# Attention steps of a fused attention and convolution kernel: one key tile at a time to the end, in place of two at a time from step 32

## The chip, the cores and the metric

The kernel runs on one core of a Trainium2 chip. The metric is device time in microseconds for one launch. The engines of the core are named as in the profile: PE is TensorE (PEld is its weight load), DVE is VectorE, ACT is ScalarE, POOL is GpSimd, SP is SyncE, which issues most DMAs here.

## The reference

Two stages, one behind the other. The first is attention in which a query sees only the keys that were routed to the same cluster; the second is a projection, a circular convolution along the sequence (written as a product of Fourier transforms), a gate and a last projection. Sizes: batch 4, 8 heads, sequence 768, head size 64, 16 clusters per head, model size 512.

```python
# q, k, v: (4, 8, 768, 64); centroids: (8, 16, 64); all float32
q_assign = argmax(einsum('bhsd,hcd->bhsc', q_n, c_n), -1)     # q_n, k_n, c_n: of length 1
k_assign = argmax(einsum('bhsd,hcd->bhsc', k_n, c_n), -1)
mask = q_assign[:, :, :, None] == k_assign[:, :, None, :]
scores = where(mask, q @ k.T / sqrt(64), -1e9)
attn = softmax(scores, -1)
x = (attn @ v).transpose(0, 2, 1, 3).reshape(4, 768, 512)

proj = x @ w_proj                                             # (512, 1536)
x1, x2, x3 = proj[..., :512], proj[..., 512:1024], proj[..., 1024:]
x2_conv = irfft(rfft(x2, axis=1) * rfft(filter_fft, axis=0), axis=1)
out = (x1 * x2_conv * x3) @ w_out                             # (4, 768, 512)
```

## The kernel before

**Groups, pairs and steps.** The 32 heads (4 batches of 8) are cut into 8 groups of four heads; two groups make a batch. A group has two pairs of heads, and a pair has six key tiles of 128. So the attention is a list of 8 x 2 x 6 = 96 steps, numbered `i` from 0 to 95, and a step is one key tile of one pair.

**A step.** `scores` (lines 383 to 392) computes for each of the two heads (`hp`) the transposed scores of one key tile against all 768 queries: two matmuls into one PSUM tile `ps` of two banks (line 387), then Exp by ACT into an SBUF tile `p` (line 391). The cluster mask is inside the matmul, since the routing's one-hot rows are appended to q and k in the tiles `aug`. There are two `ps` tiles, and eight `p` tiles that are used in turn. `values` (lines 394 to 411) multiplies by V: four matmuls in the source, eight in the profile, since the operands are float32 (line 402), with 64 columns of weights for each head, into the one PSUM tile `o`; and DVE adds `p` to a running sum per head (line 409).

**The end of a pair.** `take` lets ACT copy `o` to SBUF (lines 415 and 416). `finish` sums the denominators over the partitions on PE (line 424), sends them through DRAM to have them inverted and spread (lines 435 to 450: small DMAs, and lines 441 and 442 on DVE), scales the output on DVE (line 455), and stores it for the second stage: sum and difference on DVE (lines 488 and 489) and a bfloat16 copy on ACT (line 490).

**Routing.** `routing(n + 1)` is a generator that prepares the next group while group n is in its steps: it transposes q and k in chunks on PE (line 303), copies them on ACT (line 305) and into `aug` (lines 313 and 314), multiplies by the centroids (line 319, copied in line 321), transposes back (line 332), finds the maximum and the one-hot rows on DVE (lines 334 to 345), transposes these (line 351), and sends them into `aug` by DMA (lines 364 and 368). It yields after each chunk. It also starts the loads of the group after.

**Hyena.** The second stage of a finished batch is a generator of units too (`units`): projection (line 503), forward transform (lines 282 and 286) with DVE's products (line 554) and POOL's sums (line 557), gate (line 508, to ACT in line 568 or DVE in line 570), inverse transform (line 520) with lines 577, 537, 538 and 539, and the last projection (line 525, copied in line 587). Batches 0, 1 and 2 are interleaved with the steps from i = 32, 56 and 80 on; batch 3 comes alone at the end. In steps 0 to 6 units of table building stand in their place. All units, and routing from the second group on, share two PSUM banks `pf`.

**The order.** The order of instructions on each engine is that in which the Python code emits them. `attend(j)` emits the scores of step j for one head, then the other, and after each one it lets routing (`lead`) advance by one unit, by two on every other call where its argument `more` is true, and then lets `conv` (tables or Hyena) advance until the work done, counted in estimated microseconds, has caught up with a due time of 1.65 per `attend`. `later` and `tick` hold back things such as the end of a pair until the same count has moved on. The main loop is:

```python
if i < TWO:
    attend(i + 1, False)
    values(i)
elif i % 2 == 0:
    if i == TWO:
        attend(i + 1, True)
    attend(i + 2, True)
    attend(i + 3, True)
    values(i)
    values(i + 1)
```

With `TWO = 32`, steps 0 to 31 go one by one, with the scores one step ahead. From step 32 on, two steps of scores are emitted and then the P times V of the two steps before them, back to back: 16 matmuls of line 402 in one block.

Of the kernel before, what the change touches and what calls it, by code (L numbers as in the profile page):

```python
# [30 lines left out]
def kernel(  # L31
# [677 lines left out]
    def attend(i, more):  # L709

        due[0] += 1.65
        for hp in range(2):
            scores(i, hp)
            tick(0.35)
            calls[0] += 1
            if unit(lead) == 0.0 or (more and calls[0] % 2):
                unit(lead)
            if not conv:
                due[0] = min(due[0], paid[0] + 0.8)
            while conv and paid[0] + 0.4 < due[0] - 0.8 * (1 - hp) and unit(conv):  # L720
                pass
# [6 lines left out]
            later(2.5, pairs[n, pr].finish_on_pe if i == len(steps) - 1 else pairs[n, pr].finish)  # L728


    TWO = 32
    for hp in range(2):
        scores(0, hp)
    for i, (n, pr, sk) in enumerate(steps):
# [8 lines left out]
        if i % 24 == 8 and b > 0:  # L743
            conv.append(Hyena(b - 1, *xu[b - 1]).units())
# [6 lines that stand above are left out]
# [44 lines left out]
```

## Time and profile before

| | |
|---|---|
| median of the runs | 518.72 us (518.3 to 519.14, 2 runs) |
| the profiled execution: time, span | 518.3 us, 516.5 us |
| mean granted TensorE clock | 0.943 |
| PE busy | 421.0 us (82%) |
| DVE busy | 324.6 us (63%) |
| ACT busy | 288.8 us (56%) |
| POOL busy | 114.7 us (22%) |
| line 402, P times V on PE | 768 matmuls, 144.0 us |
| line 387, scores on PE | 384 matmuls, 94.4 us |
| line 391, Exp on ACT | 192, 153.8 us, mean 819 ns |
| line 409, sums on DVE | 160, 157.1 us |

The span runs from the first to the last instruction; the time of the execution has 1.8 us more around it. The busy time of PE is that of matmuls, which overlap a little, so that the price of a block is better read from the start of one block to the start of the next. In lines of the timeline the columns are start and length in us, engine, source line, operation, what is written and read, shapes and count; in brackets is the idle time of the engine before the line and what ended it.

### The profile page before, as it was taken

To read this page: it belongs to the slowest core of one execution; us is meant where nothing else is said; L and a number is where in the kernel's file an instruction comes from. 1 tells how busy PE (TensorE), PEld (TensorE's weight loads), DVE (VectorE), ACT (ScalarE), POOL (GpSimd) and SP (SyncE) were. 2 spreads that over 40 slices of the span, in tenths; PEclk is the share of its full clock that TensorE was granted. 3 is DMA by queue.
4 is the path that set the end of the run, shared out by engine and by line. 5 is a ranking of instruction groups with operands and counts; after the bars stand their busy time and mean duration, and the time that the engine had idled before them with its cause. 6 is when DMAs were issued, how large, how long until landed. Compare 5 with 4: busy or idle time off the path is not lost.

```text
span 516.5 us, 6689 instructions
## 1 busy us (share of the span) xinstructions
PE 421.0 (82%) x2426; PEld 184.4 (36%) x2426; DVE 324.6 (63%) x445; ACT 288.8 (56%) x475; POOL 114.7 (22%) x119
## 2 busy tenths in 40 slices
PE   4268999899796878988699876997679988978973
PEld 3133344334243433443244422443224433323521
DVE  6822887776829475565926678571683597564653
ACT  3569679679554755375456742666455736324211
POOL 7208202003006301121100413112040061111331
PEclk9669999899899898999699997999999999999988
DMA  9954827037010620135031620022004010103003
GB/s 176 237 123 93 159 76 197 19 101 171 15 49 7 148 61 33 32 92 124 30 126 32 155 63 30 1 60 65 1 32 155 2 31 0 33 0 124 1 0 122
DMA packets 67417, 38.43 MB, mean 74 GB/s; under 512 B 56060, under 2 KB 62648, under 8 KB 67384
## 3 DMA queue, kind: packets, MB, share of 16 engines
q1 hardware_dynamic: 64616, 34.99, 26.3%
q0 software_dynamic: 1056, 2.10, 2.3%
q10 hardware_dynamic: 1712, 0.92, 0.6%
q8 instruction: 19, 0.31, 0.3%
q14 instruction: 14, 0.11, 0.1%
HBM read 32.04 MB, written 7.85 MB: 77 GB/s over the span
## 4 chain that ended last, share of the span: by engine, by line
PE 53%; DVE 24%; ACT 9%; issue 7%; POOL 4%; DMA 1%; POOLq 0%; DVEq 0%; ACTq 0%; SPq 0%
PE o L402 19%; PE ps L387 8%; DVE acc L409 6%; PE pf L508 5%; ACT p L391 3%; PE pf L525 3%; PE pf L503 3%; PE pf L424 3%; DVE tm L554 2%; PE pf L303 2%; PE pf L520 2%; DVE osb L455 2%; ACT qkT L305 2%; POOL hy L539 1%; DVE mx L334 1%
## 5 line engine op out<-in xcount | busy, mean ns | idle before, releaser
L391 ACT ACTIVATE p<-ps 128x768 f32<-128x768 f32 x192 | 153.8, 819 | 81.8 <-PE ps L387 71.7
L402 PE MATMUL o<-p,vraw 128*64 128x384 f32 (+1 forms) x768 | 144.0, 512 | 0.4 <-ACT osb L416 0.4
L409 DVE TENSOR_TENSOR acc<-acc,p 128x768 f32<-128x768 f32 x128 | 123.5, 1021 | 5.1 <-ACT p L391 5.1
L387 PE MATMUL ps<-aug 128*128 128x384 bf16 (+1 forms) x384 | 94.4, 337 | 14.6 <-ACT p L391 8.0
L402 PEld LDWEIGHTS o<-p,vraw 128*64 128x64 f32 x768 | 51.6, 141 | 70.1 <-issue 68.6
L314 POOL CAST aug<-qkT 64x768 bf16<-64x768 f32 x32 | 33.0, 1035 | 133.9 <-ACT qkT L305 131.4
L387 PEld LDWEIGHTS <-aug 128*128 128x128 bf16 (+1 forms) x384 | 31.1, 99 | 77.9 <-issue 65.5
L539 POOL TENSOR_TENSOR hy<-yy,x 128x768 bf16<-128x768 f32 x12 | 25.8, 2149 | 126.5 <-DVE yy L538 126.5
L557 POOL TENSOR_TENSOR hy<-tm 128x512 bf16<-128x512 f32 x18 | 26.1, 1468 | 103.2 <-DVE tm L554 103.2
L409 DVE TENSOR_TENSOR acc<-p,p 128x768 f32<-128x768 f32 x32 | 33.6, 1087 | 21.0 <-PE pf L424 12.7
L508 PE MATMUL pf<-xT,wpj 128*128 128x384 bf16 x192 | 38.2, 330 | 7.1 <-ACT x L568 3.0
L554 DVE TENSOR_TENSOR tm<-pf,hm 128x512 f32<-128x512 f32 x36 | 22.7, 681 | 19.0 <-PE pf L282 18.1
L508 PEld LDWEIGHTS <-wpj 128*128 128x128 bf16 x256 | 24.8, 98 | 27.2 <-issue 10.7
L570 DVE TENSOR_TENSOR x<-pf,x 128x384 f32<-128x384 f32 x24 | 13.2, 555 | 31.6 <-PE pf L508 31.6
L303 PE MATMUL pf<-ident,qkraw 128*128 128x128 f32 x168 | 28.2, 286 | 5.0 <-ACT qkT L305 4.8
L305 ACT COPY qkT<-pf 128x384 f32<-128x384 f32 x56 | 26.4, 489 | 2.0 <-PE pf L303 1.7
L490 ACT CAST xT<-osb 128x768 bf16<-128x768 f32 x16 | 13.4, 835 | 24.1 <-DVE osb L455 20.1
L303 PEld LDWEIGHTS pf<-ident,qkraw 128*128 128x128 f32 x168 | 21.2, 146 | 14.4 <-ACT qkT L305 8.4
L334 DVE TENSOR_REDUCE mx<-pf 128x24 f32<-128x384 f32 x16 | 8.9, 554 | 25.6 <-PE pf L332 25.6
L520 PE MATMUL pf<-inv,hy 128*128 128x384 bf16 (+1 forms) x112 | 19.7, 338 | 5.7 <-DVE x L570 2.8
L525 PE MATMUL pf<-wout,hy 128*128 128x512 bf16 x72 | 19.6, 406 | 5.0 <-POOL hy L539 4.0
L415 ACT COPY osb<-o 128x384 f32<-128x384 f32 x16 | 7.7, 480 | 28.5 <-PE o L402 28.5
(152 smaller groups left out, 464.3 us busy)
## 6 DMA issues: line engine op xcount, KB each, us to landing
qkraw<-in_k_dram SPq DMA_DIRECT2D x32, 192.0 KB
vraw<-in_v_dram SPq DMA_DIRECT2D x8, 768.0 KB
qkraw<-in_q_dram SPq DMA_DIRECT2D x30, 192.0 KB
rb<-dr SPq DMA_DIRECT2D x30, 192.0 KB
out_dram<-tm SPq DMA_DIRECT2D x11, 512.0 KB
hy<-in_moe_filter_fft_dram SPq DMA_DIRECT2D x4, 384.0 KB
wpj<-in_moe_w_proj_dram POOLq DMA_DIRECT2D x1, 1536.0 KB, 11.5
od<-ohT SPq DMA_DIRECT2D x7, 192.0 KB
```

The source lines that it names most:

```text
L303: nc.tensor.transpose(tps[:, ts(t, 128)], qr[:, 3 * ch + t].rearrange("p h d -> p (h d)"), ident)
L305: nc.scalar.copy(qkT[z][:, ch], tps[:, :384])
L314: nc.gpsimd.tensor_copy(augs[aset][1][D:, z], qf[D:])
L387: nc.tensor.matmul(sps[:, ch, :384], self.aug[hp][:K, 2 * self.pr + 1, ts(sk, 128)], self.aug[hp][:K, 2 * self.pr, ts(ch, 384)], start=Tru ...
L391: nc.scalar.activation(p[:, :S].rearrange("p (a b) -> p a b", a=2), sps[:, :, :384], Act.Exp, scale=0.125)
L402: nc.tensor.matmul(self.o[64 * hp:64 * hp + 64, ch, :384 + ch], vv[:, 2 * self.pr + hp, sk * D:(sk + 1) * D], pb[hp][sk][:, 384 * ch:384 * ...
L409: nc.vector.tensor_tensor(acc[hp], a, pb[hp][sk][:, :S], op=Alu.add)
L508: nc.tensor.matmul(ps, wpj[:, kt, off + dt * 128:off + dt * 128 + 128], self.xT[:, kt, ts(ch, 384)], start=(kt == 0), stop=(kt == ND - 1))
L520: nc.tensor.matmul((pe, po)[e], self.y[lo:hi, i, cs, ts(dt, 128)], inv[lo:hi, row], start=(n == 0), stop=(n == 3))
L525: nc.tensor.matmul(ps, self.y2[:, kt, ts(t, 128)], wout[:, kt], start=(kt == 0), stop=(kt == ND - 1))
L539: eng.tensor_tensor(self.y2[:, dt], yy.rearrange("p t c -> p (t c)"), self.gate[dt], op=Alu.mult)
L554: nc.vector.tensor_tensor(tm[r][:, cs], ps, hm[:, i, 2 * r + cs], op=Alu.mult)
```

## The change

One constant is changed. All 96 steps take the first branch of the loop: the scores of one step, then P times V of the step before. The second branch is never entered, and `more` is always false, so routing advances by one unit per call.

```diff
-    TWO = 32
+    TWO = 96
     for hp in range(2):
         scores(0, hp)
     for i, (n, pr, sk) in enumerate(steps):
...
         if i < TWO:
             attend(i + 1, False)
             values(i)
```

On PE, what was emitted ahead of P times V of steps 36 and 37 as (S: the two score matmuls of one head, with the lines of the units between) `S 303 303 S 303 S 303 424 303 S 303 508`, then 16 of line 402, becomes `S 303 282 S 303`, eight of line 402, `424 S 303 286 S 303 286`, eight of line 402. Routing of a group then reaches its one-hot transposes (line 351) three steps later, as in the first 32 steps. The last unit of Hyena's attention-time work also shifts by a little, since the paired form calls `attend` once more at its end.

## Prediction

> **What bounds the kernel now.** I read the page first: busy shares, clock, the chain that ended last.
>
> ```profile
> PE 421.0 (82%) x2426; PEld 184.4 (36%) x2426; DVE 324.6 (63%) x445; ACT 288.8 (56%) x475; POOL 114.7 (22%) x119
> ...
> PEclk9669999899899898999699997999999999999988
> ...
> PE 53%; DVE 24%; ACT 9%; issue 7%; POOL 4%; DMA 1%; POOLq 0%; DVEq 0%; ACTq 0%; SPq 0%
> ```
>
> PE is the fullest engine and holds over half of the chain; DVE comes second. So PE time and PE waits are the currency, and the question is what the change does to each. The changed loop covers steps 32 to 95; the trace puts them at about 145 to 462 us. Over that window the windows view gives PE 267.08 us busy of 317.00, DVE 203.00, ACT 174.58: PE stands still for 49.9 us.
>
> Next, the timeline of PE in both kinds of step, for the price of a P times V block (line 402). First two single steps from the early part of the run, which has the form that the change spreads:
>
> ```profile
> 67.24 1.51 PE L402 MATMUL o<-p,vraw 128*64 128x384 f32 x8
> 68.68 0.82 PE L387 MATMUL ps<-aug 80*128 80x384 bf16 x4
> 69.44 1.51 PE L402 MATMUL o<-p,vraw 128*64 128x384 f32 x8
> ```
>
> Then a paired step, from the part that the change rewrites:
>
> ```profile
> 266.56 2.80 PE L402 MATMUL o<-p,vraw 128*64 128x384 f32 x16
> 269.30 0.50 PE L387 MATMUL ps<-aug 80*128 80x384 bf16 x2
> 269.63 1.03 PE L503 MATMUL pf<-wpj,uT 128*128 128x512 bf16 x4
> ```
>
> Read starts, not durations. A block of 8 takes 68.68 - 67.24 = 1.44 us, a block of 16 takes 269.30 - 266.56 = 2.74 us: two singles cost 0.14 us more than a pair. Two score matmuls ahead of other full-width work take 269.63 - 269.30 = 0.33 us, so four should take 0.66, but four ahead of P times V take 69.44 - 68.68 = 0.76 us: entering a block costs 0.10 us.
>
> Third, the waits of PE in 145 to 462 us, with who ended them (us in total, times, longest):
>
> ```profile
> PE pf L286 <- DVE tm L554: 7.3, 5, 2.7
> PE pf L351 <- DVE oh L345: 5.8, 4, 2.2
> PE pf L303 <- ACT qkT L305: 4.6, 8, 0.9
> PE pf L332 <- ACT sim L321: 4.0, 4, 1.0
> ...
> PE ps L387 <- ACT p L391: 2.5, 5, 0.6
> ```
>
> The whole list adds to 49.1 us in 317, or 15%. The same view over 60 to 141 us, single steps with routing but without the Hyena units, adds to only 6.1 us in 81 (7.5%), of which 3.9 is scores waiting for Exp. That wait is the one I follow last. In a single step (timeline, all engines):
>
> ```profile
> 97.13 0.83 ACT L490 CAST xT<-osb 128x768 bf16<-128x768 f32 x1 [1.94 <-DVE osb L455]
> ...
> 98.73 0.48 PE L387 MATMUL ps<-aug 80*128 80x384 bf16 x2 [1.96 <-ACT p L391]
> ```
>
> The copy of line 490 sits at the head of ACT's queue until DVE has done two sums and line 455; both Exps of the next step are queued behind it, both score buffers fill, and PE stops for 1.96 us. In a paired step the same wait is hidden:
>
> ```profile
> 376.14 2.81 PE L402 MATMUL o<-p,vraw 128*64 128x384 f32 x16
> ...
> 377.19 0.83 ACT L490 CAST xT<-osb 128x768 bf16<-128x768 f32 x1 [1.93 <-DVE osb L455]
> ...
> 378.88 0.50 PE L387 MATMUL ps<-aug 80*128 80x384 bf16 x2
> ```
>
> ACT waits as long (1.93), but PE is inside a block of 16.
>
> **The change part by part.** The base is the profiled execution, 518.3 us (span 516.5 plus 1.8 around it), 0.42 below the median of the runs, 518.72. All 96 steps become single. No matmul, Exp, sum, copy or DMA is added or removed; the order changes on every engine.
>
> *Blocks of P times V.* Steps 32 to 95 are 32 pairs, so 32 more blocks. Each costs 0.14 + 0.10 = 0.24 us: 32 x 0.24 = +7.7 us, all on PE. I see nothing that hides it where PE is busy; where PE would have waited anyway it is free, so its lower end is 0.
>
> The Trainium skill, page "TensorEngine Tiling (Array Packing)", section "Key Properties", speaks against the change: switching to another tiling mode drains the engine, and these blocks (128x64 weights) are a mode of their own between 128x128 ones. It gives no price there; "TensorE: Matmul & The Clock Gate", Part 2, puts the drain at about 128 cycles, at 2.4 GHz an estimate of 0.053 us, and two per block would make 3.4 us in place of the row's 7.7. The row decides.
>
> *Scores that wait for Exp of the same buffer.* Attending two steps in a row issues four score groups on two buffers before any P times V. Single steps put P times V between. Take the 2.5 us away; bounds -2.5 to 0.
>
> *Routing.* In pairs every other call advances routing twice, so two transposing chunks come back to back and the third waits for the copies. Waits of lines 303, 319 and 332 on ACT's copies and on line 335 add to 11.4 us in the window, and are absent from 60 to 141 us. In that stage ACT is nearly full, though (16.66 us busy of 18.30 between 76.7 and 95 us), and now Hyena's copies join, with two PSUM banks shared. I take a third back, -3.8; bounds -11.4 to 0. The one-hot transposes (line 351) waited 5.8 us in four routings; in single steps 1.8 in two. For four, -(5.8 - 3.6) = -2.2; bounds -5.8 to 0.
>
> *Routing ends later.* It is spread over three more steps, and with it go SP's loads of the next q and k, line 364 and line 368. In a single group the spread was issued at 104.1 us and the scores that need it came after 111; the new steps are longer, so there is more room. Cost 0; if the cover were gone, PE would stand still for as long as the landing is late. On SP's queue the small transfers of the divisors (435 to 450) now go between these loads; DVE already waits for them (30.0 us in the run) in places where PE mostly runs on. Cost 0, and up to +4 for four divisor waits of 1 us.
>
> *Hyena's evictions on DVE.* Sums come two at a time (1.82 us) in place of four (3.55), so an eviction queued behind them is 1.7 us less late; against that, the new DVE order puts lines 455, 488 and 489 (1.0 + 0.6 + 0.5 us) between two evictions in the gating steps, and the next inverse matmul needs both banks. Lines 282, 286, 508, 520 and 525 wait 25 us in the window; I leave that as it is, with bounds of -10 (six or so bursts shortened by 1.7) and +8 (four such places at 2.1).
>
> *Line 490 without its cover.* In the new order it comes ten times in steps 36 to 90, each time with a single block behind it. What shields PE is the other work between two score groups, priced by rows (three-matmul chunk of 332: 0.33; 282: 0.65; 508: 0.65; 503: 0.86; 520: 1.25; six of 286: 0.84). Taking 1.96 less that work, step by step: 36: 0.66; 42: 0.65; 48: 0.06; 54: 1.30; 60: 1.10; 66: 0.46; 72: 0.66; 78: 0; 84: 0.24; 90: 0.01. That is +5.1 us; bounds 0 and 10 x 1.96 = +19.6.
>
> *Clock.* Stretches in which PE worked half the time or less were followed by half clock: 95 to 99.5 us (2.33 busy), then 99.5 to 102.9 at 0.50; 191 to 195 (1.00 busy), then 195 to 198.5 at 0.51. Such a stretch costs up to 1.7 us. Both kernels have such holes; cost 0, bounds -8 and +8 (five stretches lost or gained).
>
> "TensorE: Matmul & The Clock Gate", Part 1, asks for an idle window of some 3.4 us before the clock halves; here a longest single gap of 1.96 us was enough, so by the page new short holes would cost nothing extra, and by the row they would. The row decides.
>
> Sum: +7.7 - 2.5 - 3.8 - 2.2 + 5.1 = +4.3, so 522.6 us.
>
> **The rivals.** *Line 490 bares PE* (slower). ACT in order, two score buffers, no long block. For it: 1.96 us at 98.73, and the like at 136.14 with 1.46 more on line 351 after it. Against: Hyena units now lie between. All ten bare: 19.6 in place of 5.1, 518.3 + 18.8 = 537.1 us. It decides (over +2%) from six of ten on: 6 x 1.96 = 11.8, with the other terms' -0.8 is +11.
>
> *Smoother steps* (faster). If PE's waits fell to the single stage's 7.5%: 317 - 49.1 + 7.7 = 275.6, / 0.925 = 298, so 19 less: 499.3 us. For it: halved bursts on DVE, one routing chunk per call. Against: the quiet stage has no Hyena work, and 25 us of the waits are Hyena's own.
>
> *The blocks cost nothing.* The 0.24 us falls into waits that PE has anyway: 522.6 - 7.7 = 514.9 us. For it: 15% of waits. Against: most blocks in the timeline follow PE work without a gap.
>
> **How the numbers follow.** The sum above 0.50, own range 515 to 528; blocks free 0.12; line 490 0.28; smoother 0.10. Within 2% (10.4 us, about what a measurement of this kernel can tell from no change) are the first two: 0.62; slower 0.28, faster 0.10. The range takes half of the faster case off below and goes to the full price of line 490 above: 508 to 538.
>
> **What would show it.** Right: 96 blocks of 8 with 1.44 us to the next start; the wait of scores on Exp sits after line 490 and nowhere else; lines 303 and 332 wait less than 11.4 us together. Wrong: a gap of about 2 us behind each line 490 (first rival); PE waits under 30 us in the loop (second); PE busy time that grows by 7 us while the span stays (third). A wait that I have priced nowhere, such as line 387 on a DMA, would break the sum.

## The result, and the profile after

504.31 us median (504.3 to 504.32, 2 runs) against 518.72: a ratio of 0.9722, 95% interval 0.968 to 0.9764, so 14.4 us faster. The forecast was 522.6 in a range of 508 to 538: the wrong side. The times below are medians, and each ratio is to the kernel before, run on the same chip. Its median lay between 518.7 and 521.0 us in these rounds, so a difference between two experiments is read from their ratios, as a share of 518.72 us, where it matters. Of the four runs of e3 below, two took 532 and 533 us, and its ratio is that of the other two.

The page of the changed kernel, the lines that were shown of before:

```profile
PE 420.5 (84%) x2426; PEld 179.2 (36%) x2426; DVE 336.5 (67%) x445; ACT 290.3 (58%) x475; POOL 119.2 (24%) x119
...
PEclk9769999989979898989999998999999989998998
...
PE 61%; DVE 22%; issue 6%; ACT 5%; POOL 4%; DMA 1%; POOLq 0%; DVEq 0%; SPq 0%; ACTq 0%
```

PE does the same matmuls in a shorter span (502.5 in place of 516.5 us) and now makes 61% of the chain. The waits of PE in the changed loop, 145 to 440 us:

```profile
PE pf L520 <- DVE x L570: 4.9, 5, 2.2
PE pf L282 <- DVE tm L554: 4.9, 3, 3.5
PE pf L286 <- DVE tm L554: 3.7, 2, 3.0
PE pf L286 <- DVE cand L335: 3.5, 1, 3.5
...
PE pf L508 <- DVE cand L335: 2.7, 1, 2.7
...
PE pf L332 <- DVE cand L335: 1.0, 1, 1.0
```

What has gone is routing: lines 303, 319 and 332 waited 11.4 us before and wait 1.7 now, line 351 went from 5.8 to 0.2, and the scores (line 387) from 2.5 to nothing. What has stayed are waits of Hyena's matmuls. Part of them is still owed to routing: 6.2 us of lines 286 and 508 end with line 335, which is DVE's work on routing's tile in the shared banks `pf`.

A count of PE's time over the whole span, from its records: idle 88.8 us before, 75.7 after (-13.1); work at half clock 39.2 against 34.5 us, of which half is loss (-2.3); all work, with half-clock time counted half, 401.1 against 402.8 us (+1.7). That is -13.7 of the span's -14.0. A difference of a few us in all work says little: e1 below, with the same blocks as the kernel before, has 398.1 us. By place: from the start of the block of step 31 to the start of the last matmul of line 402 the time fell from 316.7 to 298.3 us, and what comes behind it grew from 58.8 to 62.8, since single steps call `attend` once less and leave a batch of units over.

The block itself is as it was priced (231.16 to 232.60 is 1.44 us):

```profile
231.16 1.51 PE L402 MATMUL o<-p,vraw 128*64 128x384 f32 x8
232.60 0.50 PE L387 MATMUL ps<-aug 80*128 80x384 bf16 x2
```

### The profile page after: what moved, and what is told of

Read it like the earlier page. It is cut to its first block, busy times and chain, and to the rows that moved or that the text cites. A ratio compares the mean times of both kernels' runs of the same rounds, so it can differ in the third digit from the quotient of the medians.

```text
span 502.5 us, 6673 instructions
## 1 busy us (share of the span) xinstructions
PE 420.5 (84%) x2426; PEld 179.2 (36%) x2426; DVE 336.5 (67%) x445; ACT 290.3 (58%) x475; POOL 119.2 (24%) x119
## 4 chain that ended last, share of the span: by engine, by line
PE 61%; DVE 22%; issue 6%; ACT 5%; POOL 4%; DMA 1%; POOLq 0%; DVEq 0%; SPq 0%; ACTq 0%
PE o L402 22%; PE ps L387 10%; DVE acc L409 6%; PE pf L508 5%; PE pf L525 3%; PE pf L503 3%; PE pf L520 3%; DVE tm L554 3%; PE pf L424 3%; PE pf L303 3%; POOL hy L539 2%; DVE osb L455 2%; ACT p L391 2%; PE pf L319 1%; PE pf L286 1%
## 5 line engine op out<-in xcount | busy, mean ns | idle before, releaser
L402 PE MATMUL o<-p,vraw 128*64 128x384 f32 (+1 forms) x768 | 151.2, 516 | 0.4 <-ACT osb L416 0.4
L409 DVE TENSOR_TENSOR acc<-acc,p 128x768 f32<-128x768 f32 x128 | 136.7, 1113 | 6.6 <-ACT p L391 6.5
L402 PEld LDWEIGHTS o<-p,vraw 128*64 128x64 f32 x768 | 48.6, 140 | 68.7 <-issue 65.4
L314 POOL CAST aug<-qkT 64x768 bf16<-64x768 f32 x32 | 36.0, 1131 | 142.0 <-ACT qkT L305 139.9
L387 PEld LDWEIGHTS <-aug 128*128 128x128 bf16 (+1 forms) x384 | 28.9, 99 | 90.3 <-issue 80.8
L409 DVE TENSOR_TENSOR acc<-p,p 128x768 f32<-128x768 f32 x32 | 36.4, 1175 | 25.2 <-PE pf L424 10.4
L520 PE MATMUL pf<-inv,hy 128*128 128x384 bf16 (+1 forms) x112 | 19.6, 338 | 8.0 <-DVE x L570 6.1
L313 ACT CAST aug<-qkT 64x768 bf16<-64x768 f32 x28 | 23.5, 839 | 0.0
L428 ACT COPY rb<-pf 128x384 f32<-128x384 f32 x16 | 7.7, 480 | 22.5 <-PE pf L424 22.5
```

Of the source, the lines that this page charges most:

```text
L314: nc.gpsimd.tensor_copy(augs[aset][1][D:, z], qf[D:])
L387: nc.tensor.matmul(sps[:, ch, :384], self.aug[hp][:K, 2 * self.pr + 1, ts(sk, 128)], self.aug[hp][:K, 2 * self.pr, ts(ch, 384)], start=Tru ...
L402: nc.tensor.matmul(self.o[64 * hp:64 * hp + 64, ch, :384 + ch], vv[:, 2 * self.pr + hp, sk * D:(sk + 1) * D], pb[hp][sk][:, 384 * ch:384 * ...
L409: nc.vector.tensor_tensor(acc[hp], a, pb[hp][sk][:, :S], op=Alu.add)
L520: nc.tensor.matmul((pe, po)[e], self.y[lo:hi, i, cs, ts(dt, 128)], inv[lo:hi, row], start=(n == 0), stop=(n == 3))
```

## The experiments

The change does three things at once: it cuts blocks of 16 into blocks of 8; it slows routing down to one unit per call; and by the missing call of `attend` it puts Hyena's units one batch later. With the blocks go two more: the scores are emitted one step ahead (e4 and e6 ask about that), and DVE's sums come in twos (e8). The experiments take these apart. I call routing with `more` true fast, without it slow.

**Pace alone, in pairs (e1).**

```diff
-                attend(i + 1, True)
-            attend(i + 2, True)
-            attend(i + 3, True)
+                attend(i + 1, False)
+            attend(i + 2, False)
+            attend(i + 3, False)
```

> Blocks of 16 stay (steps in pairs), but routing advances by one unit per call, as in the changed kernel. Theory A (pace of routing): what PE got back are the waits of routing's chunks, 11.4 us on lines 303, 319 and 332 and 5.8 us on line 351 in the kernel before, and they came from two chunks per call; so most of it comes back here too, without the 7.7 us for 32 more blocks: about -14 us, near 504 us, and lines 303, 319 and 332 wait under 4 us together. Theory B (short steps): the gain comes from cutting the step in two, so that DVE's sums come two at a time; then this kernel stays within 4 us of the kernel before, 515 to 523 us.

Measured 499.16 us, ratio 0.9622 (0.9587 to 0.9658): 19.6 us faster, more than the whole change. Theory A holds in pairs.

**Blocks alone, with fast routing (e2).** `TWO = 96`, and `attend(i + 1, i >= 32)` in the single branch.

> All steps single, as in the changed kernel, but from step 32 on routing advances by two units on every other call, as in the kernel before. Theory A (pace of routing): the chunks of lines 303, 319 and 332 wait for their copies again (8 us or more), and the blocks cost their 7.7 us: 515 to 525 us. Theory B (short steps): close to the changed kernel, 502 to 509 us.

519.22 us, 1.0024 (0.9983 to 1.0066): with fast routing, single steps bring nothing. Theory B falls as the main cause.

**The price of a block (e3).**

```diff
-    def attend(i, more):
+    def attend(i, more, hold=False):
...
-            scores(i, hp)
+            if not (hold and hp):
+                scores(i, hp)
...
-            attend(i + 3, True)
+            attend(i + 3, True, hold=True)
             values(i)
+            scores(i + 3, 1)
             values(i + 1)
```

> The kernel before with one thing moved: the last of the four score groups of a paired step goes between the two P times V, so that each block of 16 becomes two of 8; routing's pace, Hyena's units and DVE's order stay. If PE pays for a block as it was priced, 32 x 0.24 us: +7.7 us, 526 us. If the price falls into waits that PE has anyway: 518 to 521 us. If what made the changed kernel fast is a finer mixture on PE alone: below 514 us.

1.0116 (1.0057 to 1.0174), so +6.0 us (3 to 9). The price of 7.7 lies within the interval. The edit does a little more than cut blocks: the last Exp of each paired step now stands behind the copies of that call's units in ACT's order, and no run takes the two apart.

**Scores two ahead in single steps (e4).** `attend(i + 2, False)` from step 32 on, with one call more at its start.

> The changed kernel, but from step 32 on the scores are emitted two steps ahead of P times V in place of one, as they are in paired steps. If the distance of the scores plays no part: within 3 us of the changed kernel, 501 to 508 us. If a part of the gain comes from freeing the p tiles earlier (four in use in place of eight; here six): half of what Exp waited for DVE's sums in the kernel before, 5.3 us in all, so up to 3 us slower. If two steps ahead shields PE better from line 490: up to 5 us faster, by way of fewer waits of line 387 on Exp.

493.68 us, 0.9516 (0.9478 to 0.9554): 10.6 us faster than the changed kernel, which neither side expected. The call that was added also brings Hyena's units one batch earlier, so the next run keeps that and drops the distance.

**Units one batch earlier (e5).**

```diff
+            if i == 32:
+                due[0] += 1.65
             attend(i + 1, False)
             values(i)
```

> The changed kernel with one addition: at step 32 the due time of Hyena's units is raised by 1.65 once, as the extra call of attend in the paired form and in the kernel with scores two ahead does. From there on PE's order of forms is that of the kernel with scores two ahead (493.7 us), only the scores themselves are those of one step ahead. If the 10.6 us between that kernel and the changed one (504.3) come from units that the changed kernel leaves for after the loop (62.8 us after the last P times V, against 58.1): 499 to 501 us, and the rest is the distance of the scores. If the distance of the scores is all: 503 to 505 us. If the place of the units is all: 492 to 495 us.

493.24 us, 0.9485 (0.9451 to 0.9518). The place of the units is all of it; the distance of the scores plays no part that can be seen. This kernel beats the kernel before by 27 us and the changed one by 12. Behind the last P times V it needs 58.0 us (62.8 in the changed kernel); the other 7 us are in the loop.

**Scores two ahead everywhere (e6)**, with the units as in e5.

> The kernel with scores two ahead and single steps (493.7 us), with the scores two ahead in steps 0 to 31 too. In those steps PE waits for Exp behind line 490 twice (1.96 us each), for line 351 after one of them (1.46), and half clock follows both times (10.2 us of it, up to 5 us lost). If the distance of the scores shields PE from line 490: about 8 us faster, 484 to 488 us, and no wait of line 387 on Exp behind line 490 in steps 12 to 31. If the distance does not matter there: 492 to 495 us.

494.51 us, 0.9502 (0.9466 to 0.9538). Nothing is won: PE's view of waits from 60 to 145 us still has 3.9 us of scores behind Exp.

**The same pace in bursts (e7).** In pairs, two units of routing on odd calls, none on even ones.

> Steps in pairs; routing advances by one unit per call on average, as in the kernel with pairs and slow routing (499.2 us), but as two units on every other call and none on the calls between. If two chunks of routing in a row are what costs (they hold both PSUM banks and wait for ACT's copies): most of the 19.9 us comes back, 512 to 519 us, with lines 303, 319 and 332 waiting 8 us or more. If what costs is that routing's chunks are packed into fewer calls and leave other calls without it, somewhere between: 503 to 510 us. If only the moment at which routing ends counts: 498 to 501 us.

501.44 us, 0.9639 (0.9606 to 0.9671), beside 0.9622 of e1: within the intervals. Two chunks in a row, the mechanism that I had priced, cost next to nothing, and at the slower mean pace lines 303, 319 and 332 wait 5.1 us although their chunks still come in twos. What counts is the mean pace, or what goes with it, the moment at which routing ends: the third expectation, which named that moment, was missed by 0.4 us. No run holds one of the two and moves the other, such as fast routing that begins later.

**DVE's sums early, in pairs (e8).** The sums of step i are emitted between the two calls of `attend`, those of i + 1 after the second.

> The kernel with pairs and slow routing (499.2 us), with DVE's sums of a step emitted before P times V, two after the first and two after the second attend of the pair, so never four in a row; PE's and ACT's order stay. It asks why single steps with scores two ahead (493.7 us) beat pairs although they pay 32 more blocks. If DVE's bursts of four sums are the reason: 494 us or less (5.5 us, and up to 7.7 more for the blocks saved). If not: 498 to 501 us.

496.06 us, 0.9531 (0.9494 to 0.9569): 3 us less than e1 by the medians, 4.7 by the ratios, with intervals that just miss each other. The time lies between the two expectations: bursts of four sums cost something, perhaps not the 5.5 us asked for.

**Pace and place (e9, e10, e11, e12).** e9 is e2 with the units early, as in e5; e10 is e1, and e11 the kernel before, with `due[0] -= 1.65` at step 32; e12 is e5 with 3.3.

> Single steps, routing fast (two units on every other call) and Hyena's units one batch early: beside the same with slow routing (493.2 us). If routing's pace is the cause whatever the place of the units: 508 to 515 us, 15 to 22 more. If pace and place only shift two kinds of work against each other, and a good meeting is luck: a difference under 6 us, or of the other sign, 488 to 499 us.

> Pairs, slow routing, and Hyena's units one batch late, so that they lie as in the changed kernel: beside the same with the units in their usual place (499.2 us). The place of the units was worth 11 us in single steps (504.3 against 493.2). If that is the longer end of the run and a worse meeting in any form: 506 to 511 us. If it was an accident of single steps: the end alone, about 4 us, 502 to 504 us.

> The kernel before with Hyena's units one batch late: pairs, fast routing. It completes the table of pace and place in pairs. If pace is the cause in either place, it is 15 us or more slower than pairs with slow routing and late units: 518 to 530 us. If the 19.9 us of pace were an accident of the usual place: within 6 us of that kernel, 500 to 512 us.

> Single steps, slow routing, and the units two batches early (3.3 in place of 1.65). If work taken from behind the loop is what helps, a second batch brings some 4 us more: 488 to 491 us, with under 55 us from the last P times V to the end. If the first batch was worth 11 us because it happened to lie well: 493 us or more, up to 504.

| ratio to before (us) | units early | units late |
|---|---|---|
| pairs, fast | 1 (518.7, before) | 0.9883 (513.4, e11) |
| pairs, slow | 0.9622 (499.2, e1) | 0.9765 (507.5, e10) |
| single, fast | 0.9896 (513.8, e9) | 1.0024 (519.2, e2) |
| single, slow | 0.9485 (493.2, e5) | 0.9722 (504.3, after) |

The intervals are 0.3 to 0.4% to each side. Pace is worth 3.8% in pairs with early units, 1.2% in pairs with late ones, 4.1% and 3.0% in single steps: 6 to 21 us, and always the same way. But e11 speaks against a fixed price: its 513.4 us are far below the 518 to 530 expected if pace costs the same in either place, and 5.9 us above e10, within the 6 us of the other expectation, by which the large effect was an accident of the usual place. The sign of pace holds in all four forms, its size does not. Single against pairs is worth -1.0% (early units) and +1.4% (late) with fast routing, -1.4% and -0.4% with slow: 7 us faster to 7 us slower, by what it meets. The place of the units moves a kernel by up to 2.4%, and not always the same way, so it is a matter of how they meet; a second batch (e12: 494.89 us, 0.9512) brings nothing more.

**How does pace cost? DVE's order (e13, e14, e15, e16).** In the fast kernels PE waits 11 to 18 us for the one-hot rows (lines 345 and 353), in the slow ones 0 to 5, and in the kernel before DVE has the end of a pair (455, 488, 489) between these two lines. e13 is the kernel before with `later(18, scale)` in place of 15; e15 is e5, and e16 is e9, with the same; e14 is e5 with the end of every second pair emitted between lines 345 and 353.

> The kernel before (pairs, fast routing) with the end of a pair, lines 455, 488, 489 and 490, put off by three more units of the count, so that in all four routings of the loop DVE does line 353 ahead of it in place of behind it. If the collision on DVE is how pace costs: waits for lines 345 and 353 fall from 11.3 us to under 6 and the time by 5 to 12 us, 507 to 514 us. If the collision is only where the wait shows, and pace costs by packing routing away from Hyena's units: within 3 us of the kernel before, 516 to 522 us.

> The fast version (single steps, slow routing, units early, 493.2 us) with the end of every second pair held back until routing has its one-hot rows and emitted between line 345 and line 353, four times in the loop. If the collision is how pace costs: each time DVE is 2 us later with line 353 and more where units queue behind, 8 us or more in all, 500 to 506 us, with 6 us or more of waits for line 353. If not: 492 to 496 us.

> The fast version (single steps, slow routing, units early, 493.2 us) with the end of a pair put off by three units of the count; there is no collision to take away in the loop. If moving line 455 has no effect of its own: 491 to 496 us. In steps 19 and 31 line 490 now comes behind the one-hot chain, so PE's 1.96 us waits there may go or move: up to 5 us faster.

> Single steps, fast routing, units early (513.8 us), with the end of a pair put off by three units of the count; DVE's order then has line 353 ahead of line 455 in all four routings, though two sums per step still lie between lines 345 and 353. If the collision with the end of a pair is how pace costs: 500 to 508 us. If the sums between, or the packing, are enough: 511 to 516 us.

e13 527.06 us, 1.0142 (1.0094 to 1.019); e14 494.49, 0.9513 (0.9481 to 0.9545); e15 511.39, 0.9841 (0.9809 to 0.9872); e16 518.36, 0.9969 (0.9932 to 1.0005). The collision is not shown to be the way. Put in (e14), it costs nothing, and PE waits only 1.1 us for line 353 there. Taken out, it does not help: in e13 the waits of PE for the one-hot rows fell from 11.3 to 6.1 us, but those of lines 303, 319 and 332 rose from 11.4 to 24.3, and in e16 they went from 12.8 to 3.2 and from 8.1 to 16.4. So e13 and e16 moved other waits along with the collision, and e14 comes nearest to testing it alone. That e15 lost 18 us by a shift of three units in the count was in no theory; ACT's waits at line 490 rose from 12.0 to 20.1 us in it (145 to 445 us), which led to the last pair of runs; yet from e9 to e16 they fell from 39.4 to 18.9 us, and e16 is the slower one.

**Line 490 off the head of ACT's queue (e17, e18).**

```diff
-            nc.scalar.copy(xT[:, kt], self.osb[:, :S])
+            osb = self.osb
+            if self.bg == (B - 1, 1):
+                nc.scalar.copy(xT[:, kt], osb[:, :S])
+            else:
+                later(4.0, lambda: nc.scalar.copy(xT[:, kt], osb[:, :S]))
```

> The kernel before (pairs, fast routing, 518.7 us) with ACT's copy of line 490 emitted 4.0 units of the count after line 455, about a step later, so that DVE has done line 455 before the copy comes to the head of ACT's queue. In steps 0 to 31 this takes away two waits of 1.96 us, one of 1.46 us and the half clock behind them: 5 to 8 us. If line 490 is also how the pace of routing costs: 10 us or more on top, so 497 to 504 us, and the stretch from step 31 to the last P times V shrinks from 316.7 to below 305 us. If not: 510 to 515 us, and that stretch stays above 312 us.

> The fast version (single steps, slow routing, units early, 493.2 us) with the same change. The first 32 steps give 5 to 8 us here too. If line 490 also costs in the loop (12.0 us of waiting on ACT before it, but only 0.7 us of scores that wait for Exp): up to 4 us more. 481 to 488 us; 490 us or more would say that the waits behind line 490 only move.

516.84 us, 0.9943 (0.9917 to 0.997), and 493.55, 0.9519 (0.9457 to 0.9581). ACT no longer waits there (0.9 us behind line 455 in either); 3 us are won in the one and nothing in the other. PE's waits from 60 to 145 us in e17:

```profile
PE pf L351 <- DVE oh L345: 6.2, 2, 3.5
PE pf L282 <- DVE cand L335: 0.6, 1, 0.6
PE o L402 <- ACT osb L416: 0.4, 2, 0.2
```

The 3.9 us of scores behind Exp are gone, and line 351 waits 6.2 in place of 1.8: the wait moved to the next thing that DVE owes.

**What stays open.** The way by which mean pace costs is not shown by an experiment. What remains is packing: fast routing presses its chunks into fewer calls, and the other work falls elsewhere. One of the stretches looked at speaks for it. Before, around the routing of the last group, first the stretch with its chunks, then the one behind it (busy us of PE, PEld, DVE, ACT, POOL with counts, then clock):

```profile
345.70:366.70 21.00, 14.33 (x98) 6.39 (x96) 6.27 (x10) 14.61 (x26) 3.57 (x4) 1.00 0.20 58
366.70:389.20 22.50, 17.14 (x101) 7.13 (x100) 18.51 (x25) 10.64 (x17) 5.70 (x2) 1.00 0.06 19
```

After, the stretch with the chunks of the same routing and the one behind it:

```profile
332.80:358.00 25.20, 23.71 (x154) 10.83 (x154) 18.32 (x23) 19.03 (x33) 6.75 (x6) 1.00 0.15 49
358.00:380.00 22.00, 18.68 (x108) 7.23 (x104) 17.21 (x23) 11.62 (x19) 2.38 (x1) 1.00 0.25 85
```

Here, with fast routing, DVE is 30% busy while routing's chunks run and PE 68%; behind them DVE is 82% busy and PE 76%. Since `unit` counts routing as work done, Hyena's units are kept out of the first stretch and crowd into the second. With slow routing they mix: DVE 73 and 78%, PE 94 and 85%. Around the routing one group earlier the contrast is much weaker, before:

```profile
287.60:308.00 20.40, 16.26 (x101) 6.55 (x101) 12.67 (x20) 12.57 (x22) 3.32 (x4) 1.00 0.50 114
308.00:330.00 22.00, 16.30 (x86) 6.78 (x87) 16.60 (x21) 7.96 (x13) 7.97 (x5) 0.84 0.05 18
```

and after:

```profile
276.30:303.00 26.70, 22.73 (x142) 9.92 (x140) 19.40 (x23) 17.06 (x30) 10.90 (x8) 1.00 0.42 105
303.00:318.50 15.50, 14.00 (x82) 5.53 (x82) 13.38 (x19) 7.67 (x14) 3.22 (x2) 0.89 0.09 26
```

DVE goes from 62 to 75% before and from 73 to 86% after; PE is at 80 and 74%, then at 85 and 90%. There both stretches are merely fuller after, which is the gain itself as much as a reason for it. So packing fits e7 (bursts do not change the mixture) and the small effect of single cures, but it is argued, from the last group above all: no run changed the mixture alone.

## Why the prediction was wrong, point by point

- *Blocks, +7.7.* Right in kind, the size not settled. Starts are 1.44 us apart as priced. All of PE's work, with half-clock time counted half, grew by 5.0 us from e1 (64 blocks) to e5 (96), from 398.1 to 403.1, but by only 1.7 from the kernel before to the changed one; e3 gave 6.0 (3 to 9).
- *Scores waiting for Exp, -2.5.* Right: none in the new loop.
- *Routing, -3.8 and -2.2.* This is the step that failed. I named the right knob (routing by two units on every other call) and took a third of its own waits; the waits of these lines fell by 9.6 and 5.6 us, and pace measured alone is worth 6 to 21 us, by the form, in place of the 6.0 of the two terms. Two errors: I doubted the quiet stage, which had shown that these waits vanish at a slow pace; and I took two chunks in a row for the reason, which e7 refutes as the main one. In e1 the waits of these lines, 351 with them, fell from 17.2 to 4.8 us, 12.4 of the 19.6 that were won. In which places the rest was won is not shown.
- *Routing ends later, 0.* Right: no score in the loop waits for a DMA.
- *Hyena's evictions, 0.* Near: lines 282, 286, 508, 520 and 525 waited 25 us before and wait 30 after.
- *Line 490 without its cover, +5.1.* Wrong: scores wait 0.0 us for Exp in the new loop. The wait is there on ACT (21.2 us against 15.6 before, 145 to 445 us), but PE stands elsewhere, on an eviction that DVE owes:

```profile
189.05 0.83 ACT L490 CAST xT<-osb 128x768 bf16<-128x768 f32 x1 [2.96 <-DVE osb L455]
...
190.58 0.56 DVE L335 TENSOR_TENSOR cand<-pf,mx 128x384 bf16<-128x384 f32 x1
191.05 0.55 DVE L334 TENSOR_REDUCE mx<-pf 128x24 f32<-128x384 f32 x1
191.19 0.82 PE L508 MATMUL pf<-xT,wpj 128*128 128x384 bf16 x4 [2.65 <-DVE cand L335]
```

  e17 and e18 say that taking this wait away wins 3 us or nothing. The rival built on it, with 0.28, had no ground in this loop.
- *Clock, 0.* It gave: mean granted clock 0.943 of 516.5 us loses 29.4 us, 0.949 of 502.5 loses 25.6.
- *The call of `attend` less.* Named in the text on the code, priced nowhere. In slow single steps it cost 12 us (e5), in pairs with fast routing later units win 6 (e11).

The rival "smoother steps", with 499.3 us and 0.10, came closest. It held one chunk per call and halved bursts on DVE; the first is the large one (e1), the second small (e8, 3 to 5 us). That its number lies near the measured one is partly luck: it leaves out the late units, which cost 12 us here. The sign given for it, under 30 us of PE's waits in the loop, was missed by a little (32.4). The evidence against it, that Hyena's waits are its own, was largely true and beside the point.

Sum after the fact, by the ratios: pace -19.6 (e1), single steps -7.1 (e5 against e1), late units +12.3: -14.4 us. These are steps from cell to cell of the table, so they must add up to the measured change and confirm nothing, and another way gives other terms: late units -6.1 (e11), pace -6.1 (e10 against e11), single steps -2.2. The three act on each other, and none has a price of its own; the price of the blocks is inside the step to single steps.

## What to carry to other kernels

Where several streams of work share one order, ask first how a change moves the streams against each other, not only what it costs at its own line. The busy time of each engine in the stretch with the stream and in the one behind it is a place to look; read it for every stretch, since one group alone showed the strong contrast here. A diff of one constant can turn several knobs (here block size, pace and place); list every argument that it flips, price or test each alone, and then in combination: the place of the units changed sign with the form. Waits of single lines are poor prices in such a loop: taken away, they came back one queue further on (e17), while a shift of three units in the count, which touched no line's own cost, moved the time by 18 us (e15).

## What the runs showed of the hardware that was not expected

Of the 14 us, 2 to 4 are less half clock. It does not go with PE's idle time as a whole: the kernel before has 88.8 us idle and 39.2 us of PE's work at half clock, e5 66.9 and 29.4, but e2 82.8 and 52.4 and e7 80.0 and 27.6. Half clock began 8 times before, 6 times in e5, 11 in e2 and 5 in e7 (counted without the first 40 and the last 10 us), and this goes with how close the holes lie. The granted clock is recorded in steps of 3.41 us. In all twenty profiles, counted in the same way, half clock followed every step at full clock in which PE was busy for under 1.40 us, none with over 2.03 us, and some of those between. No long gap is needed: in the kernel before, the half clock at 171.2 us follows 1.69 us of work with no gap above 1.05 us.

DVE's sums go with what POOL does: four take 3.55 us from 153.01 us on in the profile before, and 5.96 from 165.47 on, beside lines 557 and 314 on POOL. Of the 128 sums of that form, the 101 with nothing on POOL beside them took 0.90 to 0.96 us, the other 27 took 1.30 on average and up to 2.03. With Hyena mixed in more evenly, the mean sum (line 409, all but the first of a pair) rose from 1021 to 1113 ns, and the kernel was still faster.
